# Packed query loads and a changed order of steps in a one-core linear-attention and mixture-of-depths kernel

## Chip, cores and metric

The kernel runs on one core of a Trainium2 chip. The metric is the time of one execution on the device in microseconds (us); smaller is better. All numbers below are of this one core.

## What is computed

The reference is a block-wise linear attention with a decay for each head, followed by a layer that sends the 128 best tokens of each of four batches through a two-matrix network. Cut to what matters, with B=4 batches, H=8 heads, S=768 tokens, D=64:

```python
for b in range(nb):                       # 12 blocks of 64 tokens
    intra = einsum('bhic,bhjc->bhij', qb, kb) * Dmask      # lam ** (i - j), i >= j
    intra = einsum('bhij,bhjd->bhid', intra, vb)
    inter = einsum('bhid,bhde->bhie', qb * lam_pow, kv_state)
    out[:, :, sl] = intra + inter
    kv_state = lam_block * kv_state + einsum('bhsd,bhse->bhde', kb * rev_pow, vb)
x = out.transpose(0, 2, 1, 3).reshape(B, S, 512)
scores = x @ w_gate
for b in range(B):
    top = the 128 tokens of batch b with the highest scores
    y = relu(x[b, top] @ w1) @ w2          # 512 -> 1024 -> 512
    out[b, top] = x[b, top] + sigmoid(scores[b, top])[:, None] * y
```

## The kernel before

The work is cut into 24 groups of 128 tokens (two blocks of 64), six groups to a batch; NT is 6, NG is 24. The engines' queues are written out by hand, in program order: the loop over g at L591 is one step for each group, and each step holds pieces of several groups, so that the engines overlap.

**Loads.** `load(g)` (L61) issues three DMAs on SyncE's queue (SP), one each for q, k and v of a group: 128 tokens on 128 partitions, 8 heads of 64 numbers beside each other, so every piece that is contiguous in memory is 256 bytes. Groups 0 to 2 are loaded ahead of everything, 3 to 5 in the prologue, and step g issues `load(g + 6)`; each name has 7 buffers. From step 4 to step 11 a step also issues `load_weights` (L81) behind its loads on the same queue: the four quarters of `w1_sb` in steps 4 to 7, the four of `w2_sb` in steps 8 to 11. Stores of the output go through ScalarE's queue (L315).

**A group's attention.** `keys_decayed` (L182) multiplies k by powers of the decay on GpSimd (tile `kd`). `transposes` (L191) turns q and k with TensorE: four 128x128 transposes of q into the PSUM tile `tq`, four of k into the upper halves of the two PSUM tiles `pu`; ScalarE copies them out as `qT` (L203) and `kT` (L206). `queries_decayed` (L209) makes `qs` on GpSimd. `scores` (L218) and `from_states` (L271) are 64x64 products on quarters of the array into `po`; `masked` (L229) multiplies the scores by the mask on VectorE (`p`); `from_scores` (L286) adds the rest of `po`. `state_products` (L241) fills the lower halves of `pu`; `decay_state` (L252, GpSimd, `decayed`) and `next_state` (L260, VectorE, `state`) carry the state on. `pu` has a single buffer (L54), so `state_products` of the next group waits until `next_state` and the copies of `kT` have read it. A 64x64 product in float32 stands in the profile as two matmuls and two weight loads.

**Order in a step.** Step g runs, on TensorE, `from_scores(g)`, `scores(g+1)`, `from_states(g+1)`, `state_products(g+2)`, perhaps an expert's `gate`, `transposes(g+2)`, then the pieces put into this step, and the transposed row of scores `row` (L340, tile `pb`). On GpSimd it runs `decay_state`, `keys_decayed(g+3)`, `queries_decayed(g+2)`, `decay_state`, and what pieces issue there.

**Choice of tokens and expert.** `gate_scores` (L325), `row`, `compare` and `compare_older` count for each token how many beat it. `places` (L394) has two parts: `ranks` (VectorE, tile `hit`) and `tokens` (six small products `pk` on TensorE, then the token numbers `tok` on VectorE). `expert` (L430) gathers the chosen rows into `xs` with an indirect DMA on GpSimd (`fetch`, L438), transposes them (`gate`, L446, `pt`), and has 16 pieces: eight of `hidden` (tile `ph`, L478, which reads all four quarters of `w1_sb`) and eight of `back` (`py`, L492); the last writes `y` back with an indirect DMA (L504). `plan(b)` (L525) lays these into later steps by `put(step, key, piece)`: for batches 0 to 2, with s = 6(b+1), ranks go to step s+1, tokens and the gather to step s+1 with keys 5 and 6, the gate to step s+3 and the pieces to steps from s+3 on. For the last batch all of it follows step 23. `row`, `tq`, `pt`, `pk`, `ph` and `py` share two PSUM banks, handed out in turn by `bank` (L163); an expert's `ph` or `py` holds one of them.

Of the kernel before, what the change touches and what calls it, by code (L numbers as in the profile page):

```python
# [17 lines left out]
def kernel(  # L18
# [12 lines left out]
    nc = tc.nc  # L31
# [11 lines left out]
    NGR = (CAP + 127) // 128  # L43
    NG = B * NT
    AHEAD = 6
    assert D == 64 and H % 2 == 0 and S % L == 0 and HD == 512 and F % 512 == 0
    assert 0 <= CAP < S

# [12 lines left out]
    def load(g):  # L61
        b, c = divmod(g, NT)
        rows = slice(c * L, (c + 1) * L)
        tiles = []
        for name, src in (("qn", q), ("kn", k), ("vn", v)):
            t = ld.tile([128, H, D], FP32, name=name)
            nc.sync.dma_start(out=t[:], in_=src[b, :, rows, :].rearrange("h p d -> p h d"))
            tiles.append(t)
        loaded[g] = tiles
# [46 lines left out]
    if CAP % 128:  # L116
# [4 lines left out]
            out=in_cap[:], in_=in_cap[:], compare_op=ALU.is_gt, fill=0.0,  # L121
            base=CAP % 128, pattern=[[0, 1]], channel_multiplier=-1,
        )
    half = [slice(0, C), slice(C, 2 * C)]

    mask = const.tile([128, 2, NHP, C], FP32, name="mask")
# [34 lines left out]
    def bank(shape, name, hold=False):  # L163

        tag = next(t for t in banks if t not in held)
        banks.remove(tag)
        banks.append(tag)
        if hold:
            held.append(tag)
        return ps_m.tile(shape, FP32, name=name, tag=tag)  # L170
# [11 lines left out]
    def keys_decayed(g):  # L182
        kd = att.tile([128, H, D], FP32, name="kd")
        nc.gpsimd.tensor_tensor(  # L184
            out=kd[:], in0=loaded[g][1][:],
            in1=kpow[:].rearrange("p a b -> p (a b)").unsqueeze(2).broadcast_to([128, H, D]),
            op=ALU.mult,
        )
        kds[g] = kd

    def transposes(g):  # L191

        tq = bank([128, NHP, L], "tq")
        tk = [u[:, NHP * D :].rearrange("p (a i) -> p a i", i=L) for u in us[g]]
        W = NHP // 2
        for i, dst in ((0, tq), (1, None)):
            for hp in range(NHP):
                nc.tensor.transpose(  # L198
                    dst[:, hp, :] if i == 0 else tk[hp // W][:, hp % W, :],
                    in_=loaded[g][i][:, 2 * hp : 2 * hp + 2, :], identity=ident[:],  # L200
                )
        qT = att.tile([128, NHP, L], FP32, name="qT")
        nc.scalar.copy(out=qT[:], in_=tq[:])  # L203
        kT = att.tile([128, NHP, L], FP32, name="kT")
        for i in range(2):
            nc.scalar.copy(out=kT[:, i * W : (i + 1) * W, :], in_=tk[i])  # L206
        qTs[g], kTs[g] = qT, kT

    def queries_decayed(g):  # L209
        qs = att.tile([128, NHP, L], FP32, name="qs")  # L210
        nc.gpsimd.tensor_tensor(  # L211
            out=qs[:], in0=qTs[g][:], in1=qpow[:].rearrange("p a c i -> p a (c i)"), op=ALU.mult
        )
        qss[g] = qs
# [14 lines left out]
    def masked(g):  # L229
        p = att.tile([128, 2, NHP, C], FP32, name="p")  # L230
        nc.vector.tensor_tensor(  # L231
            out=p[:].rearrange("p a b i -> p a (b i)"),
            in0=pos[g][:, :, 1].rearrange("p a b i -> p a (b i)"),
            in1=mask[:].rearrange("p a b i -> p a (b i)"), op=ALU.mult,
        )
        ps_[g] = p

    def start_u(g):
        us[g] = [ps_u.tile([128, 512], FP32, name=f"pu{c}") for c in range(2)]

    def state_products(g):  # L241
        vn, kd = loaded[g][2], kds.pop(g)
        for hp, hh, c in quarters():
            if c == 1 and g % NT == NT - 1:
                continue
            h = 2 * hp + hh
            nc.tensor.matmul(  # L247
                us[g][c][half[hh], hp * D : (hp + 1) * D], lhsT=kd[half[c], h, :],
                rhs=vn[half[c], h, :], start=True, stop=True, skip_group_check=True,
            )  # L250
# [86 lines left out]

    rows_, beatens, toks, upto = {}, {}, {}, {}

    def row(g):  # L340

        b, t = divmod(g, NT)
        if t == 0:
            rows_[b] = mod.tile([128, S], FP32, name="sc_row", tag="sc_row")
            beatens[b] = mod.tile([128, NT, NT + 1], FP32, name="beaten")
            nc.gpsimd.memset(beatens[b][:], 0.0)
            upto[b] = {n: n for n in range(NT)}
        pb = bank([128, L], "pb")
        nc.tensor.transpose(
            pb[:], in_=scs[b][:, t : t + 1].broadcast_to([128, 128]), identity=ident[:]  # L350
        )
        nc.scalar.copy(out=rows_[b][:, t * L : (t + 1) * L], in_=pb[:])

        cmp = mod.tile([128, S], BF16, name="cmp")
        nc.vector.scalar_tensor_tensor(
            out=cmp[:, :L], in0=pb[:], scalar=scs[b][:, t : t + 1], in1=not_before[:],
            op0=ALU.is_equal, op1=ALU.mult, accum_out=beatens[b][:, t, NT : NT + 1],
        )

# [158 lines left out]
    def put(step, key, piece):  # L518
        later.setdefault(step, []).append((key, piece))
# [5 lines left out]
    def plan(b):  # L525
        last = b == B - 1
        s = (b + 1) * NT
        ranks, tokens = places(b)
        if last:

            def last_row():
                compare_older(NG - 1)
                row(NG - 1)
                compare(NG - 1)
                ranks()

            put(s, 35, last_row)
            put(s, 85, tokens)
        else:
            ranked[s + 1] = ranks  # L540
            put(s + 1, 5, tokens)
        for i in range(NGR):
            s = max(s, busy_until[0])
            fetch, gate, pieces = expert(b, i)
            if s + 3 >= NG:
                s = max(s, NG)
                put(s, 86, fetch)
                put(s + 1, 0, gate)
                for j, piece in enumerate(pieces):
                    put(s + 2, j, piece)  # L550
                busy_until[0] = s + 3
                continue
            put(s + 1, 6, fetch)
            gates[s + 3] = gate

            whole = s + 9 <= NG
            counts = [2, 3, 3, 3, 3, 2] if whole else [1, 1, 1]
            assert len(pieces) == 16
            where = [(s + 3 + i, 10 * (j + 1)) for i, n in enumerate(counts) for j in range(n)]
            where = [w for w in where if w[0] < NG]  # L560
            where += [(NG, 10 * (j + 1)) for j in range(len(pieces) - len(where))]
            for (step, key), piece in zip(where, pieces):
                put(step, key, piece)
            busy_until[0] = s + 6 if whole else NG

    keys_decayed(0)
    start_u(0)
    transposes(0)
    queries_decayed(0)
    keys_decayed(1)  # L570
    state_products(0)
    next_state(0)
    decay_state(1)
# [1 line left out]
    decay_state(2)  # L575
    for g in range(3, AHEAD):
        load(g)
    start_u(1)
    transposes(1)
    queries_decayed(1)  # L580
    keys_decayed(2)
    scores(0)
    from_states(0)
    state_products(1)
    masked(0)
    next_state(2)
    decay_state(3)
    next_state(3)
# [2 lines left out]
    for g in range(NG):  # L591
        if g + AHEAD < NG:
            load(g + AHEAD)
        if 0 <= g - NT + 2 < n_w:
            load_weights(g - NT + 2)
        if g >= 2 * NT and kept:
            store_kept()
        if g + 2 < NG:
            decay_state(2 * g + 4)
        if g + 3 < NG:  # L600
            keys_decayed(g + 3)
        from_scores(g)
        outputs(g)
        if g + 1 < NG:
            scores(g + 1)
            from_states(g + 1)
            masked(g + 1)
        if g in ranked:
            ranked.pop(g)()
        if g % NT == 0 and g > 0 and NGR:  # L610
            compare_older(g - 1)
        if g + 2 < NG:
            start_u(g + 2)
            state_products(g + 2)
        if g in gates:
            gates.pop(g)()
        if g + 2 < NG:
            transposes(g + 2)
            queries_decayed(g + 2)
            next_state(2 * g + 4)  # L620
            decay_state(2 * g + 5)
        gate_scores(g)
        pieces = later.pop(g, [])

        rows = [r for r in {NG - 2: [g - 1, g], NG - 1: []}.get(g, [g - 1]) if r >= 0 and NGR]
        if g % NT == 0:
            for r in rows:
                row(r)
        else:
            in_order(pieces)  # L630
            for r in rows:
                row(r)
        if g + 2 < NG:
            next_state(2 * g + 5)
        for r in rows:
            compare(r)
        if g % NT == 0:
            in_order(pieces)
        if g % NT == NT - 1 and NGR:
            plan(g // NT)  # L640
# [35 lines left out]
```

## Time and profile before

| | |
|---|---|
| median of 3 runs | 188.24 us (187.86 to 188.97) |
| profiled execution | 189.73 us, of which the profile's span covers 188.0 us |
| granted TensorE clock, mean | 0.962 |
| TensorE busy, matmul / weight load | 153.5 us (82%) / 124.9 us (66%), 3520 of each |
| VectorE / ScalarE / GpSimd busy | 110.6 us (59%) / 68.0 us (36%) / 103.4 us (55%) |
| DMA | 80898 packets, 32.23 MB, mean 171 GB/s; 75616 packets under 512 B |
| last chain by engine | TensorE 56%, issue 16%, GpSimd 10%, VectorE 9%, DMA 3%, ScalarE 3% |

The span starts at 0 with the first instruction. Step g begins where the 32 matmuls of L289 for group g begin: step 0 at 15.66 us, step 1 at 22.56, step 2 at 27.15, step 7 at 51.99, step 8 at 59.75, step 9 at 66.34, step 10 at 72.42, step 23 at 153.77. After 154 us TensorE works through what is left of the third expert, then the whole of the fourth. In a timeline row, the first two numbers are the start and the length, a form is out<-in, xN counts merged instructions, and the square bracket holds the idle time of that engine just before, with what ended it. "issue" means idle for no reason that the profile shows. A DMA's row is its issue; the time to landing is listed apart.

### The profile page before, as it was taken

Reading aid. Unit: us, or ns where it says so; the run is one execution under the profiler, and the core shown is the slowest. Engines: PE = TensorE matmul, PEld = TensorE weight load, DVE = VectorE, ACT = ScalarE, POOL = GpSimd, SP = SyncE. Lnnn points to the kernel's source line nnn. Section 1 sums busy time; section 2 is a strip of 40 time slices with the busy share of each in tenths; the row PEclk is TensorE's granted clock in tenths of the full one; section 3 lists DMA queues with packets and bytes.
Section 4 is the critical chain, followed back from the end, with each engine's and each line's share of the span. In section 5 each row is a group of like instructions: output and inputs, shape, how many; then the busy total and the mean of one; then the engine's idle time right before and its main releaser. Section 6 shows DMA issues by size and latency. Waiting matters only on the chain.

```text
span 188.0 us, 8090 instructions
## 1 busy us (share of the span) xinstructions
PE 153.5 (82%) x3520; PEld 124.9 (66%) x3520; DVE 110.6 (59%) x357; ACT 68.0 (36%) x185; POOL 103.4 (55%) x110
## 2 busy tenths in 40 slices
PE   0957886876674799989799599999899969989980
PEld 0737775765564699988367399995667859549630
DVE  3903345866998378757873646749957689530000
ACT  2222253643344155536225333554425533111100
POOL 4386387867876686576756933768578500111002
PEclk9999699999999579999999969999999999999999
DMA  5999999899999999998999899411121211011001
GB/s 112 223 228 216 233 250 234 196 257 239 257 266 249 274 241 266 245 250 259 344 296 225 220 250 228 104 59 61 58 56 64 112 59 59 0 56 56 0 0 56
DMA packets 80898, 32.23 MB, mean 171 GB/s; under 512 B 75616, under 2 KB 75616, under 8 KB 80864
## 3 DMA queue, kind: packets, MB, share of 16 engines
q1 hardware_dynamic: 76688, 23.34, 56.1%
q10 hardware_dynamic: 3536, 6.30, 9.8%
q0 software_dynamic: 640, 2.10, 3.4%
q8 instruction: 27, 0.44, 1.0%
q14 instruction: 7, 0.06, 0.1%
HBM read 24.38 MB, written 7.34 MB: 169 GB/s over the span
## 4 chain that ended last, share of the span: by engine, by line
PE 56%; issue 16%; POOL 10%; DVE 9%; DMA 3%; ACT 3%; POOLq 1%; ACTq 0%; DVEq 0%
PE ph L478 11%; PE py L492 10%; PE pu L247 7%; PE tq L198 6%; PE po L289 6%; POOL qs L211 6%; PE po L278 5%; PE po L224 5%; PE pu L198 3%; POOL decayed L257 3%; ACT qT L203 3%; DMA lam_b<-in_lam_dram 2%; DVE cmp L365 2%; DMA out_dram<-y,tok 2%; DVE state L268 1%
## 5 line engine op out<-in xcount | busy, mean ns | idle before, releaser
L211 POOL TENSOR_TENSOR qs<-qT,qpow 128x512 f32<-128x512 f32 x24 | 31.3, 1303 | 27.6 <-ACT qT L203 26.0
L257 POOL TENSOR_TENSOR decayed<-state,decay 128x256 f32<-128x256 f32 x40 | 37.1, 927 | 16.7 <-DVE state L268 13.8
L478 PE MATMUL ph<-xsT,w_sb 128*128 128x128 f32 x256 | 31.1, 278 | 0.7 <-ACT xsT L454 0.7
L268 DVE TENSOR_TENSOR state<-pu,decayed 128x256 f32<-128x256 f32 x40 | 16.9, 422 | 24.3 <-ACT kT L206 17.7
L478 PEld LDWEIGHTS ph<-xsT,w_sb 128*128 128x128 f32 x256 | 29.8, 193 | 1.1 <-ACT xsT L454 0.9
L365 DVE TENSOR_SCALAR_CACHE_REDUCE cmp<-sc_row,sc 128x128 bf16<-128x128 f32 (+3 forms) x66 | 29.9, 497 | 0.0
L492 PE MATMUL py<-w_sb,hs 128*128 128x512 f32 x64 | 29.4, 599 | 0.4 <-ACT qT L203 0.4
L203 ACT COPY qT<-tq 128x512 f32<-128x512 f32 x24 | 14.0, 585 | 42.6 <-PE tq L198 41.4
L184 POOL TENSOR_TENSOR kd<-kn,kpow 128x512 f32<-128x512 f32 x24 | 26.0, 1082 | 3.0 <-DVE kpow L138 3.0
L328 DVE CUSTOM_DVE_ANT_0 xg<-x_b,wg_b 128x512 f32<-128x512 f32 x24 | 25.9, 1077 | 0.0
L247 PE MATMUL pu<-vn,kd 64*64 64x64 f32 x704 | 20.9, 237 | 3.5 <-DVE state L268 2.8
L278 PE MATMUL po<-state,qs 64*64 64x64 f32 x704 | 18.0, 225 | 7.0 <-issue 4.5
L231 DVE TENSOR_TENSOR p<-po,mask 128x512 f32<-128x512 f32 x24 | 16.5, 687 | 10.1 <-PE po L278 10.1
L198 PE MATMUL tq<-ident,qn 128*128 128x128 f32 x96 | 17.8, 315 | 5.6 <-DMA qn<-in_q_dram 4.9
L224 PE MATMUL po<-qT,kT 64*64 64x64 f32 x768 | 17.8, 228 | 5.0 <-issue 5.0
L247 PEld LDWEIGHTS pu<-vn,kd 64*64 64x64 f32 x704 | 17.7, 147 | 4.7 <-DVE state L268 1.8
L278 PEld LDWEIGHTS po<-state,qs 64*64 64x64 f32 x704 | 15.1, 138 | 8.1 <-issue 5.1
L492 PEld LDWEIGHTS py<-w_sb,hs 128*128 128x128 f32 x64 | 11.4, 190 | 11.9 <-issue 10.8
L289 PEld LDWEIGHTS po<-vn,p 64*64 64x64 f32 x768 | 14.5, 144 | 7.0 <-issue 4.2
L224 PEld LDWEIGHTS po<-qT,kT 64*64 64x64 f32 x768 | 15.2, 141 | 5.7 <-issue 5.7
L198 PE MATMUL pu<-ident,kn 128*128 128x128 f32 x96 | 17.1, 305 | 2.0 <-DVE state L268 1.9
L289 PE MATMUL po<-vn,p 64*64 64x64 f32 x768 | 17.9, 235 | 0.3 <-DVE p L231 0.3
(53 smaller groups left out, 151.4 us busy)
## 6 DMA issues: line engine op xcount, KB each, us to landing
qn<-in_q_dram SPq DMA_DIRECT2D x24, 256.0 KB, 5.3
kn<-in_k_dram SPq DMA_DIRECT2D x24, 256.0 KB, 5.5
vn<-in_v_dram SPq DMA_DIRECT2D x24, 256.0 KB, 5.7
out_dram<-x_b ACTq DMA_DIRECT2D x18, 256.0 KB, 3.7
w_sb<-in_moe_w_dram SPq DMA_DIRECT2D x8, 512.0 KB, 5.8
out_dram<-x_b ACTq DMA_DIRECT2D x2, 768.0 KB
wg_b<-in_moe_w_gate_dram SPq DMA_DIRECT2D x1, 256.0 KB
xs<-out_dram,tok POOLq DMA_INDIRECT x4, 4.5
```

Of the source, the lines that this page charges most:

```text
L184: nc.gpsimd.tensor_tensor(out=kd[:], in0=loaded[g][1][:], in1=kpow[:].rearrange("p a b -> p (a b)").unsqueeze(2).broadcast_to([128, H, D]) ...
L198: nc.tensor.transpose(dst[:, hp, :] if i == 0 else tk[hp // W][:, hp % W, :], in_=loaded[g][i][:, 2 * hp : 2 * hp + 2, :], identity=ident[:],)
L211: nc.gpsimd.tensor_tensor(out=qs[:], in0=qTs[g][:], in1=qpow[:].rearrange("p a c i -> p a (c i)"), op=ALU.mult)
L224: nc.tensor.matmul(po[half[c], hh, 1, hp, :], lhsT=kT[half[hh], hp, half[c]], rhs=qT[half[hh], hp, half[c]], start=True, stop=True, skip_g ...
L247: nc.tensor.matmul(us[g][c][half[hh], hp * D : (hp + 1) * D], lhsT=kd[half[c], h, :], rhs=vn[half[c], h, :], start=True, stop=True, skip_g ...
L257: nc.gpsimd.tensor_tensor(out=t[:], in0=states[n][:], in1=decay[:], op=ALU.mult)
L278: nc.tensor.matmul(pos[g][half[hh ^ c], hh, 0, hp, :], lhsT=qs[half[hh], hp, half[c]], rhs=states[n][half[hh], hp, :], start=(hp == 0), st ...
L289: nc.tensor.matmul(pos[g][half[hh ^ c], hh, 0, hp, :], lhsT=p[half[c], hh, hp, :], rhs=vn[half[c], 2 * hp + hh, :], start=(hp == 0 and (2 ...
L328: nc.vector.tensor_tensor_reduce(out=xg[:], in0=x_bs[b][:, t].rearrange("p a b e -> p (a b e)"), in1=wg_b[:], scale=1.0, scalar=0.0, op0=A ...
L365: nc.vector.tensor_scalar(out=cmp[:, : cols.stop - cols.start], in0=rows_[b][:, cols], scalar1=scs[b][:, t : t + 1], scalar2=None, op0=op, ...
L478: nc.tensor.matmul(ph[:, fc % 4, :], lhsT=w1_sb[:, dc, fc * 128 : (fc + 1) * 128], rhs=keep["xsT"][:, dc, :], start=(dc == 0), stop=(dc == ...
L492: nc.tensor.matmul(py[:], lhsT=keep["hs"][:, fc, :], rhs=w2_sb[:, fc, :], start=(fc == 0), stop=(fc == NFC - 1),)
```

## The change

1. For groups 0 to 11 (`PACKED`, two batches), q is loaded in another shape: partition (hh, a, t) of the tile holds eight neighbouring tokens 8t to 8t+7 of head 2a+hh, 2 KB in one piece. It takes two DMAs of 64 partitions, one for each hh, in place of one of 128. k and v stay as they were.
2. For these groups the four transposes of q become 16 products of 64x64, on two quarters of the array (rows hh to columns hh), with the identity `ident2` as moving operand, and the copy to `qT` reads PSUM with a step of 64 elements to put the tokens in order again.
3. For groups 0 and 1, k is transposed into a `bank` tile of its own (`tk`), not into `pu`, and the prologue runs `scores(0)` ahead of `state_products(0)`, and `from_states(0)` and `masked(0)` ahead of `state_products(1)`.
4. `tokens` and `fetch` of batch 0 move from step 7 to step 8; its gate stays in step 9. Those of batches 1 and 2 stay in their step, with keys 25 and 26, so behind two pieces of `back`.
5. The `row` of groups 22 and 23 uses the `pu` tiles, not a `bank`; `start_u` is called once more for that.

```diff
+    PACKED = 2 * NT
+            if name == "qn" and g < PACKED:
+                qsrc = src[b, :, rows, :].rearrange("(a h) (t s) d -> h a t (s d)", h=2, s=8)
+                for hh in range(2):
+                    nc.sync.dma_start(
+                        out=t[half[hh]].rearrange("p s d -> p (s d)"), in_=qsrc[hh]
+                    )
+                tiles.append(t)
+                continue
...
     def transposes(g):
         tq = bank([128, NHP, L], "tq")
-        tk = [u[:, NHP * D :].rearrange("p (a i) -> p a i", i=L) for u in us[g]]
...
+        if g < PACKED:
+            for s in range(8):
+                for hh in range(2):
+                    nc.tensor.matmul(
+                        tq[half[hh]].rearrange("p a i -> p (a i)")[:, s * 64 : s * 64 + 64],
+                        lhsT=loaded[g][0][half[hh], s, :], rhs=ident2[half[hh], :],
+                        start=(s == 0), stop=True, skip_group_check=True,
+                    )
+            nc.scalar.copy(
+                out=qT[:].rearrange("p a (t s) -> p a t s", s=8),
+                in_=tq[:].rearrange("p a i -> p (a i)").rearrange(
+                    "p (s a t) -> p a t s", s=8, a=NHP
+                ),
+            )
+        else:
...
+        if g < 2:
+            tk = bank([128, NHP, L], "tk")
+            tk = [tk[:, i * W : (i + 1) * W, :] for i in range(2)]
+        else:
+            tk = [u[:, NHP * D :].rearrange("p (a i) -> p a i", i=L) for u in us[g]]
...
-    def row(g):
+    def row(g, pb=None):
...
-        pb = bank([128, L], "pb")
+        if pb is None:
+            pb = bank([128, L], "pb")
+        pb = pb[:, :L]
...
-                row(NG - 1)
+                row(NG - 1, us[NG][1])
...
-            put(s + 1, 5, tokens)
+            where = (s + 1, 25) if b > 0 else (s + 2, 5)
+            put(*where, tokens)
...
-            put(s + 1, 6, fetch)
+            put(s + 1, 26, fetch) if i > 0 or b > 0 else put(s + 2, 6, fetch)
...
     keys_decayed(0)
-    start_u(0)
     transposes(0)
     queries_decayed(0)
     keys_decayed(1)
+    scores(0)
+    start_u(0)
     state_products(0)
...
-    start_u(1)
     transposes(1)
+    from_states(0)
+    masked(0)
     queries_decayed(1)
     keys_decayed(2)
-    scores(0)
-    from_states(0)
+    start_u(1)
     state_products(1)
-    masked(0)
...
+        if g + 2 <= NG:
+            start_u(g + 2)
         if g + 2 < NG:
-            start_u(g + 2)
             state_products(g + 2)
...
-                row(r)
+                row(r, us[NG][0] if r == NG - 2 else None)
```

More of the change, by code (lines that the diff above doesn't have):

```diff
@@ L45 @@
     AHEAD = 6
+    PACKED = 2 * NT
+    half = [slice(0, C), slice(C, 2 * C)]
     assert D == 64 and H % 2 == 0 and S % L == 0 and HD == 512 and F % 512 == 0
@@ L123 @@
         )
-    half = [slice(0, C), slice(C, 2 * C)]
     mask = const.tile([128, 2, NHP, C], FP32, name="mask")
@@ L193, in transposes @@
         tq = bank([128, NHP, L], "tq")
-        tk = [u[:, NHP * D :].rearrange("p (a i) -> p a i", i=L) for u in us[g]]
-        W = NHP // 2
-        for i, dst in ((0, tq), (1, None)):
+        qT = att.tile([128, NHP, L], FP32, name="qT")
+        if g < PACKED:
[13 more added lines that the diff above has]
+        else:
             for hp in range(NHP):
                 nc.tensor.transpose(
-                    dst[:, hp, :] if i == 0 else tk[hp // W][:, hp % W, :],
-                    in_=loaded[g][i][:, 2 * hp : 2 * hp + 2, :], identity=ident[:],
-                )
-        qT = att.tile([128, NHP, L], FP32, name="qT")
-        nc.scalar.copy(out=qT[:], in_=tq[:])
+                    tq[:, hp, :], in_=loaded[g][0][:, 2 * hp : 2 * hp + 2, :], identity=ident[:]
+                )
+            nc.scalar.copy(out=qT[:], in_=tq[:])
+        W = NHP // 2
+        if g < 2:
[3 more added lines that the diff above has]
+            tk = [u[:, NHP * D :].rearrange("p (a i) -> p a i", i=L) for u in us[g]]
+        for hp in range(NHP):
+            nc.tensor.transpose(
+                tk[hp // W][:, hp % W, :], in_=loaded[g][1][:, 2 * hp : 2 * hp + 2, :],
+                identity=ident[:],
+            )
         kT = att.tile([128, NHP, L], FP32, name="kT")
@@ L347, in row @@
             upto[b] = {n: n for n in range(NT)}
-        pb = bank([128, L], "pb")
+        if pb is None:
+            pb = bank([128, L], "pb")
+        pb = pb[:, :L]
         nc.tensor.transpose(
-            pb[:], in_=scs[b][:, t : t + 1].broadcast_to([128, 128]), identity=ident[:]
+            pb, in_=scs[b][:, t : t + 1].broadcast_to([128, 128]), identity=ident[:]
         )
-        nc.scalar.copy(out=rows_[b][:, t * L : (t + 1) * L], in_=pb[:])
+        nc.scalar.copy(out=rows_[b][:, t * L : (t + 1) * L], in_=pb)
         cmp = mod.tile([128, S], BF16, name="cmp")
         nc.vector.scalar_tensor_tensor(
-            out=cmp[:, :L], in0=pb[:], scalar=scs[b][:, t : t + 1], in1=not_before[:],
+            out=cmp[:, :L], in0=pb, scalar=scs[b][:, t : t + 1], in1=not_before[:],
             op0=ALU.is_equal, op1=ALU.mult, accum_out=beatens[b][:, t, NT : NT + 1],
```

## Prediction

> **What bounds the kernel now.** I read first the page's DMA rows, then the DMA view of two windows, then the timelines around the first expert (59 to 76 us) and the prologue, then the chain of waits.
>
> The page: mean busy share of the 16 DMA engines in 40 slices of 4.7 us, then packets, MB and share by queue (q1 is SP's, q10 ScalarE's, q8 carries instructions).
>
> ```profile
> DMA  5999999899999999998999899411121211011001
> ...
> q1 hardware_dynamic: 76688, 23.34, 56.1%
> q10 hardware_dynamic: 3536, 6.30, 9.8%
> ...
> q8 instruction: 27, 0.44, 1.0%
> ```
>
> The engines are full from 5 to 118 us. SP's packets count out: 72 loads x 1024 pieces = 73,728, 128 for the gate row, 512 and 1,024 for the weights; 1,296 are left, which is 16 for each of SP's 81 DMAs.
>
> Prices, from the DMA view of 30 to 45 us (loads alone on q1) and of 125 to 165 us (quiet, stores on q10):
>
> ```profile
> q1 hardware_dynamic: 9981, 2.52, 76.6%
> ```
>
> ```profile
> q10 hardware_dynamic: 864, 1.57, 10.6%
> ```
>
> 0.766 x 16 x 15 us / 9981 = 18.4 ns for a 256-byte packet. 0.106 x 16 x 40 us / 864 = 78 ns; 96 of the 864 are the small ones (six stores x 16), about 9 ns each, so a 2 KB packet takes 87 ns.
>
> Full engines hurt only where someone waits for what they bring late. The last quarter of w1 is issued in step 7, behind the loads of group 13, and the first expert needs it in step 9. SP's timeline, the landing times in 60 to 72 us, and TensorE's timeline:
>
> ```profile
> 61.51 0.91 SPq L83 DMA_DIRECT2D w_sb<-in_moe_w_dram  x1
> ```
>
> ```profile
> w_sb<-in_moe_w_dram SPq DMA_DIRECT2D x2, 512.0 KB, 6.4
> ```
>
> ```profile
> 70.37 2.02 PE L478 MATMUL ph<-xsT,w_sb 128*128 128x128 f32 x16
> ```
>
> It lands at 61.51 + 6.4 = 67.9 and is read at 70.37: 2.5 us to spare, the smallest margin of any load I found. TensorE itself loses time in three ways. The timeline shows it waiting in the prologue and for tokens and rows:
>
> ```profile
> 12.26 0.69 PE L198 MATMUL pu<-ident,kn 128*128 128x128 f32 x2 [1.95 <-DVE state L268]
> ```
>
> ```profile
> 59.35 0.30 PE L417 MATMUL pk<-ids,hit 128*128 128x2 bf16 x6 [2.46 <-DVE hit L406]
> ```
>
> ```profile
> 96.34 0.30 PE L417 MATMUL pk<-ids,hit 128*128 128x2 bf16 x6 [0.39 <-DVE hit L406]
> ```
>
> ```profile
> 135.82 0.30 PE L417 MATMUL pk<-ids,hit 128*128 128x2 bf16 x6 [0.77 <-DVE hit L406]
> ...
> 153.51 0.32 PE L349 MATMUL pb<-ident,sc 128*128 128x128 f32 x1 [1.45 <-DVE cmp L355]
> ```
>
> And the chain of waits has stretches in which TensorE waited for nothing shown:
>
> ```profile
> 42.63 1.58 issue
> ...
> 48.48 1.29 issue
> ...
> 53.23 1.19 issue
> ...
> 105.36 2.18 issue
> ```
>
> With 80.56 (0.71) and 92.73 (1.22) these six sum to 8.2 us. From 44.2 to 49.8 and from 49.8 to 54.4 about 127 matmuls and as many weight loads pass, and q8's 27 packets are 16 KB each: these are pauses at instruction pages, 4.6 to 5.6 us apart.
>
> [...]
>
> **The change, part by part.** *The packed load.* The memory side of each half is 4 heads (98,304 numbers apart) x 16 x 2 KB; the heads cannot be merged with the 16. Its slowest dimension is 4, the tile's is 64[...], both halves on the same four engines. Each of these then carries 128/4 = 32 packets of 2 KB a group, 32 x 87 ns = 2.78 us, where it carried 64 x 18.4 ns = 1.18 us. That is 1.61 us more a group, 19.3 us for twelve; the other twelve engines get 1.18 us less. A DMA that spans all 16 (k, v, weights) lands with the slowest. So the last quarter of w1, behind all twelve packed groups, lands 19.3 us later, less the time these engines now stand idle. The table by stage (length, busy time of each engine, granted clock, DMA share, GB/s) has only these two stretches below a share of 0.97:
>
> ```profile
> 32.40:36.60 4.20, 3.61 (x123) 3.12 (x121) 3.23 (x9) 2.69 (x9) 3.45 (x5) 1.00 0.79 184
> ...
> 41.30:46.50 5.20, 3.62 (x123) 3.22 (x121) 3.56 (x9) 2.34 (x8) 4.14 (x4) 1.00 0.95 234
> ```
>
> 0.21 x 4.2 + 0.05 x 5.2 = 1.1 us idle. L478 then waits 19.3 - 1.1 - 2.5 = 15.7 us. Behind it on TensorE stand the next row and from_scores(10), so the other engines run dry.
>
> Bounds: none if k is 16; at the loaded rate of 2 KB packets (window 30 to 45, q10: 121 ns with the small ones taken off) 32 x 121 - 1180 = 2.69 us a group, 32 us. I take the quiet rate[...]. SP issues four DMAs a group instead of three[...]. As late keys also pace steps 3 to 8 (group period on four engines 2.78 + 2 x 1.18 = 5.1 us bare, 5.9 with a store of 8 x 87 ns; the steps take 4.2 to 5.5), everything earlier than the weights is under this cover.
>
> *Transposes as products.* 8 TensorE instructions become 64 a group, so 56 more. Sixteen matmuls on two quarters (L247 in group 11) took 0.46 us to the next instruction in the chain, so 32 take 0.93 against 0.60: 0.33 us x 10 groups = 3.3 us, hidden under the load wait, on the path without it. Copy to qT with a stepped read: between 0 and +0.59 us (twice the row) a group; I take 0. A gain is excluded, as the same 512 elements pass.
>
> *Prologue.* Key transposes no longer wait 1.95 us for the state. What is late next is GpSimd's own row of kd(1), decayed, qs, kd(2); that leaves about 1.0 us. Under load wait: nothing, since k and v of group 1 come later.
>
> *Tokens of batch 0.* 2.46 us on TensorE and the row that GpSimd's memset delays go. By the step lengths 51.99 to 59.75 and 59.75 to 66.34 against about 5.3, 2.0 + 1.3 = 3.3 us are at stake. But the gather now stands behind decayed of step 8, which ends at 68.5 in the old clock, 65.2 in the shortened one, lands 5 us later at 70.2, and the gate reads at 69.0: net +1.2 us (-3.3 to +3). Hidden by the wait for w1 while that is there. *Batches 1 and 2:* two back products cover the 0.39 and 0.77 us. *Rows:* 0.25 us, since sc(22) is ready at 153.2 and pb waited to 153.5. These three are behind the weights and count: -1.4 us. The order of instructions on the engines says what moves with the pieces: VectorE's tok_f and tok of batch 0 go one step down with the tokens, the gather goes past the memset of `beaten` and a step of GpSimd's work; for batches 1 and 2 GpSimd's order is as before, and masked(0) keeps its place on VectorE.
>
> Sum: 189.73 + 15.7 - 1.4 = 204.0 for an execution like the profiled one, which is 1.5 above the median of the runs: 202.5, which I round to 202.
>
> **Rivals.** *The loads do spread over 16 engines, and TensorE's pages decide.* For: [...] Ten groups x 56 = 560 instructions = 2.2 pages, at 4.9 us a page up to 10.7 us[...]. 188.24 + 5.4 + 1.2 - 1.0 - 1.4 = 192.4. [...] *The other side: loads on 16 engines relieve the fetch of instructions.* A group's q takes 8 x 87 = 0.70 us instead of 1.18, 5.8 us less by group 12; the six pauses lie before 118 us, where the queues are full; after that the chain has one of 0.43 us. 188.24 - 8.2 + 3.3 + 1.2 - 1.0 - 1.4 = 182.1. It decides from k = 8 on: 16 x 87 = 1.39 us is 0.21 above the old 1.18, within the (2.5 + 1.1)/12 = 0.3 us of slack; with k = 4 it cannot. *The edits cancel:* 188.
>
> **Numbers.** Four engines 0.61, own range 195 to 207. Low: the pauses after step 9 (0.71 + 1.22 + 2.18) go[...], and a packet takes 80 ns (2.7 us less). High: 100 ns a packet, 5.0 us more. Page-bound 0.18, relieved 0.15, cancelled 0.06. The range leaves out the relieved case and the far tails: 187 to 207. Within 0.5% is about what a measurement of this kernel can tell from no change. Faster 0.15, same 0.06, slower 0.79.
>
> **What would show it.** SP's packets: 65,744 + 24k, 65,840 with four engines, 66,128 with sixteen. A wait of L478 for w_sb near 70 us, GpSimd waiting for kn in steps 3 to 8, and a DMA share of 5 to 7 tenths, not 9, before 80 us. Wrong: 16 small packets a packed DMA, w_sb landing before 70 us.

## The result, and the profile after

| | before | changed |
|---|---|---|
| median of 4 runs, same chip | 188.13 us | 205.74 us (204.84 to 210.71) |
| ratio, 95% interval | | 1.0895 (1.082 to 1.097) |
| the same once more, in another series | 186.52 us | 204.25 us, ratio 1.0944 (1.088 to 1.101) |

The changed kernel is slower by 17.6 us; 202 with a range of 187 to 207 was forecast. Medians and ranges are of all runs; the ratios here and below compare only the runs within 1.5% of the fastest of the same kernel. The first profiled execution lasted 210.71 us, 5 us over its own median. All readings below, where the first profile is not named, are therefore from a second profile of the same program, whose execution lasted 203.34 us with a span of 201.6, against 189.73 and 188.0 before: 13.6 us more. The other 4.0 us of the 17.6 lie between executions: the one profiled before was 1.6 us above its median, this one 0.9 below the median of its series, and that median 1.5 below the first.

The DMA share by slices of 5.0 us, SP's and the instructions' queues (packets, MB, share of 16 engines), and the chain that ended last by engine (SPq is SP's queue), in which the kernel before had 56% for TensorE, 3% for DMA and nothing for SP:

```profile
DMA  1779848667796789999999999991113121011001
...
q1 hardware_dynamic: 65840, 23.34, 51.3%
...
q8 instruction: 30, 0.49, 1.1%
...
PE 39%; SPq 15%; DMA 14%; POOL 10%; issue 9%; DVE 7%; ACT 3%; POOLq 1%; ACTq 0%; DVEq 0%
```

65,840 is 65,744 + 24 x 4: four small packets a packed DMA. The forecast's k, the number of engines of one packed DMA, is 4: in the first profile, by the times of the packets from 25 to 70 us, at most five 2 KB packets of q are in flight in 99% of the time that there are any, most often four. The packets of a pair's second half, issued at 31.16 us, begin there at 34.59, as those of the first half end (34.64). From 5 to 70 us the engines together are busy 75% of the time (by slices 40 to 90%), and yet SP stands. Its timeline for two packed groups and the last quarter of w1 (the two packed DMAs of a group are merged in one row):

```profile
44.79 5.08 SPq L73 DMA_DIRECT2D qn<-in_q_dram  x2
49.97 0.41 SPq L78 DMA_DIRECT2D kn<-in_k_dram  x1
50.47 0.53 SPq L78 DMA_DIRECT2D vn<-in_v_dram  x1
51.05 3.96 SPq L73 DMA_DIRECT2D qn<-in_q_dram  x2
...
81.98 1.01 SPq L94 DMA_DIRECT2D w_sb<-in_moe_w_dram  x1
```

A pair mostly holds SP for 3.6 to 5.1 us. From the issue at 33.78 to that at 56.41 four groups take 22.63 us, 5.66 each; 5.1 bare and 5.9 with a store had been worked out. In that stretch the table by stage (length, busy time of each engine, granted clock, DMA share, GB/s) has a share of 0.70, where before it was 1.02 from 20 to 60 us:

```profile
33.78:56.41 22.63, 17.76 (x633) 15.49 (x631) 13.01 (x39) 9.44 (x28) 14.97 (x16) 0.96 0.70 170
```

The last quarter of w1 was issued at 81.98 instead of 61.51. By the times of its packets, which no row here shows, the last one ends at 86.9 us, against 67.2 before: 19.7 us later (forecast 19.3 - 1.1 = 18.2). But the first expert doesn't wait for it. TensorE's timeline in step 9:

```profile
85.27 1.08 PE L484 MATMUL pt<-ident,xs 128*128 128x128 f32 x4 [4.89 <-DMA xs<-out_dram,tok]
86.28 1.97 PE L208 MATMUL tq<-ident,qn 64*64 64x64 f32 x32
88.18 1.12 PE L232 MATMUL pu<-ident,kn 128*128 128x128 f32 x4
89.09 2.51 PE L512 MATMUL ph<-xsT,w_sb 128*128 128x128 f32 x16
```

Row L512 (L478 before) has no wait in front of it: the gathered rows were there only at 85.1 us, and the last packet of w1 had ended 2.2 us before ph. And TensorE works slowly behind that wait; the granted clock is the third figure from the right:

```profile
85.00:87.00 2.00, 1.74 (x18) 1.43 (x20) 0.70 (x2) 0.61 (x2) 0.00 (x0) 0.50 1.16 293
87.00:89.00 2.00, 2.00 (x28) 1.88 (x25) 0.32 (x2) 0.70 (x3) 0.00 (x0) 0.50 1.10 210
89.00:91.00 2.00, 2.00 (x15) 2.00 (x13) 1.41 (x3) 0.71 (x2) 1.98 (x2) 0.68 0.92 282
91.00:93.00 2.00, 2.00 (x99) 1.83 (x100) 0.95 (x5) 0.85 (x3) 0.74 (x1) 1.00 1.15 255
```

Where the time went is read from the starts of the steps (L321, before L289):

| step starts at | 2 | 5 | 7 | 9 | 10 | 14 | 16 | 23 | span |
|---|---|---|---|---|---|---|---|---|---|
| before | 27.15 | 41.37 | 51.99 | 66.34 | 72.42 | 99.36 | 113.93 | 153.77 | 188.0 |
| changed | 34.65 | 50.67 | 65.41 | 77.32 | 91.65 | 116.96 | 128.09 | 167.29 | 201.6 |
| later by | 7.5 | 9.3 | 13.4 | 11.0 | 19.2 | 17.6 | 14.2 | 13.5 | 13.6 |

Eleven us are lost up to the start of step 9, where late loads set the pace, 8.2 in step 9, and 5 of these come back by step 16. GpSimd's waits (total, times, longest) show the first part; before it waited for no kn at L184:

```profile
POOL kd L193 <- DMA kn<-in_k_dram: 20.1, 7, 5.5
```

The chain of waits shows a second way by which a late load passes on. At 57.3 a store on ScalarE's queue is released by the landing of v, whose issue SP had delayed, and the copy to qT stands behind that store. The trace gives both DMAs the same completion semaphore (a counter of landings, number 101 here): its last count for v came at 57.30 us, and the store was issued at 57.37.

```profile
50.47 6.83 DMA vn<-in_v_dram
...
57.37 0.34 ACTq L347
...
57.81 0.59 ACT qT L213
...
58.47 1.28 POOL qs L243
```

### The profile page after: what moved, and what is told of

It reads as the page before. It is cut to its first block, busy times and chain, and to the rows that moved or that the text cites. A ratio compares the mean times of both kernels' runs of the same rounds, so it can differ in the third digit from the quotient of the medians.

```text
span 209.0 us, 8773 instructions
## 1 busy us (share of the span) xinstructions
PE 167.1 (80%) x3856; PEld 137.0 (66%) x3856; DVE 110.2 (53%) x357; ACT 68.5 (33%) x185; POOL 103.0 (49%) x110
## 3 DMA queue, kind: packets, MB, share of 16 engines
q1 hardware_dynamic: 65840, 23.34, 49.6%
## 4 chain that ended last, share of the span: by engine, by line
PE 38%; SPq 17%; issue 11%; DMA 11%; DVE 10%; POOL 7%; ACT 3%; POOLq 1%; ACTq 0%; DVEq 0%
SPq L73 12%; PE ph L512 9%; PE py L526 8%; SPq L78 4%; PE pu L279 4%; DMA vn<-in_v_dram 4%; PE tq L208 3%; PE tq L221 3%; PE po L321 3%; DMA kn<-in_k_dram 3%; POOL qs L243 3%; POOL decayed L289 3%; DMA xs<-out_dram,tok 2%; PE po L310 2%; PE po L256 2%
## 5 line engine op out<-in xcount | busy, mean ns | idle before, releaser
L289 POOL TENSOR_TENSOR decayed<-state,decay 128x256 f32<-128x256 f32 x40 | 36.6, 916 | 14.9 <-DVE state L300 14.7
L512 PE MATMUL ph<-xsT,w_sb 128*128 128x128 f32 x256 | 32.0, 283 | 0.7 <-ACT xsT L488 0.7
L526 PE MATMUL py<-w_sb,hs 128*128 128x512 f32 x64 | 31.7, 632 | 0.4 <-ACT qT L224 0.4
L512 PEld LDWEIGHTS ph<-xsT,w_sb 128*128 128x128 f32 x256 | 30.7, 199 | 1.1 <-ACT xsT L488 0.9
L208 PE MATMUL tq<-ident,qn 64*64 64x64 f32 x384 | 20.8, 272 | 8.8 <-DMA qn<-in_q_dram 7.3
L208 PEld LDWEIGHTS tq<-ident,qn 64*64 64x64 f32 x384 | 19.3, 185 | 9.4 <-DVE lam_p L153 5.9
L360 DVE CUSTOM_DVE_ANT_0 xg<-x_b,wg_b 128x512 f32<-128x512 f32 x24 | 24.9, 1037 | 0.0
L213 ACT COPY qT<-tq 128x512 f32<-128x512 f32 x12 | 7.0, 585 | 50.8 <-PE tq L208 38.4
L256 PE MATMUL po<-qT,kT 64*64 64x64 f32 x768 | 16.7, 227 | 2.9 <-ACT kT L238 2.8
L321 PEld LDWEIGHTS po<-vn,p 64*64 64x64 f32 x768 | 13.6, 135 | 6.7 <-issue 3.4
L337 ACT COPY x_b<-po 64x256 f32<-64x256 f32 x48 | 17.6, 366 | 0.6
L321 PE MATMUL po<-vn,p 64*64 64x64 f32 x768 | 16.9, 226 | 0.5 <-DVE p L263 0.5
```

The costliest lines, as they stand in the source:

```text
L208: nc.tensor.matmul(tq[half[hh]].rearrange("p a i -> p (a i)")[:, s * 64 : s * 64 + 64], lhsT=loaded[g][0][half[hh], s, :], rhs=ident2[half ...
L289: nc.gpsimd.tensor_tensor(out=t[:], in0=states[n][:], in1=decay[:], op=ALU.mult)
L321: nc.tensor.matmul(pos[g][half[hh ^ c], hh, 0, hp, :], lhsT=p[half[c], hh, hp, :], rhs=vn[half[c], 2 * hp + hh, :], start=(hp == 0 and (2 ...
L360: nc.vector.tensor_tensor_reduce(out=xg[:], in0=x_bs[b][:, t].rearrange("p a b e -> p (a b e)"), in1=wg_b[:], scale=1.0, scalar=0.0, op0=A ...
L512: nc.tensor.matmul(ph[:, fc % 4, :], lhsT=w1_sb[:, dc, fc * 128 : (fc + 1) * 128], rhs=keep["xsT"][:, dc, :], start=(dc == 0), stop=(dc == ...
L526: nc.tensor.matmul(py[:], lhsT=keep["hs"][:, fc, :], rhs=w2_sb[:, fc, :], start=(fc == 0), stop=(fc == NFC - 1),)
```

## The experiments

Theory A is the forecast's: a packed load ran on four engines. Theory B: the products on TensorE, with their instructions, are what costs. Theory C: the later gather of batch 0 costs by itself. Ratios are to the kernel before on the same chip.

**1. Sixteen engines.**

```diff
-                qsrc = src[b, :, rows, :].rearrange("(a h) (t s) d -> h a t (s d)", h=2, s=8)
+                qsrc = src[b, :, rows, :].rearrange("(a h) (t s) d -> h t a (s d)", h=2, s=8)
...
-                    "p (s a t) -> p a t s", s=8, a=NHP
+                    "p (s t a) -> p a t s", s=8, a=NHP
```

> Only the order of the partitions inside a half is changed, from (head, token block) to (token block, head), and the read of the copy to qT with it: the slowest dimension of the memory side becomes 16. Theory A (the forecast: a packed load ran on four engines): SP's packets rise from 65,840 to 66,128, the pair of packed issues no longer holds SP for about 4 us, steps 1 to 9 come back to the pace of before, the last quarter of w1 lands before 70 us instead of at 87.5, and the time is 182 to 189 us. Theory B (the 56 more TensorE instructions a group and the stepped copy are what costs): nothing of that matters, 200 us or more. Theory C (the later gather of batch 0 costs by itself): the wait of pt for xs stays at 4 to 5 us, and the time is 189 to 193.

Measured: 195.31 us, ratio 1.034 (1.025 to 1.043).

```profile
q1 hardware_dynamic: 66128, 23.34, 52.6%
```

```profile
29.50 2.75 SPq L73 DMA_DIRECT2D qn<-in_q_dram  x2
32.36 0.52 SPq L78 DMA_DIRECT2D kn<-in_k_dram  x1
32.98 0.53 SPq L78 DMA_DIRECT2D vn<-in_v_dram  x1
33.56 2.82 SPq L73 DMA_DIRECT2D qn<-in_q_dram  x2
```

Sixteen small packets a DMA, 4.3 us from pair to pair in the mean of four instead of 5.7, w1 landed at 68.6, step 9 at 68.93 (2.6 after the kernel before). The copy to qT takes 587 ns, as before. So going from four to sixteen engines takes away 10 us of the 17. The edit also changes the sequence of addresses, but that did not change the price of the packets: in sum SP's took 0.526 x 16 x 194.3 = 1635 us here and 0.513 x 16 x 201.6 = 1655 us in the changed kernel. What changed is over how many engines they are spread. The time is above A's range all the same, and above C's: 3.4% stay, and in step 9 pt waits 5.3 us for xs, so C is alive. Behind that wait pt, pu and ph take 1.09, 1.04 and 2.23 us, against 0.59, 0.44 and 1.85 in the kernel before, at a clock of 1.00 (67.8 to 72.4 us).

**2. Eight engines**, by four DMAs of 32 partitions, on top of edit 1.

```diff
-                for hh in range(2):
+                for i in range(4):
                     nc.sync.dma_start(
-                        out=t[half[hh]].rearrange("p s d -> p (s d)"), in_=qsrc[hh]
+                        out=t[32 * i : 32 * i + 32].rearrange("p s d -> p (s d)"),
+                        in_=qsrc[i // 2, 8 * (i % 2) : 8 * (i % 2) + 8],
                     )
```

> As the run with sixteen, but four DMAs of 32 partitions, whose memory side has a slowest dimension of 8. Theory A: eight engines carry 16 packets of 2 KB a group, about 1.4 us against 1.18 before and 2.78 with four engines, which is inside the slack: 16 + 16 = 32 small packets a group, SP's packets 66,128 again (4 x 8 a group), and a time within 3 us of the run with sixteen (184 to 191). If the number of engines were not what counts, but the number of DMAs or of packets, it would stand near 205.

Measured: 201.26 us, ratio 1.074 (1.064 to 1.084). The packets are 66,128, as for eight engines; the time is a miss. From the chain:

```profile
31.59 3.91 DMA out_dram<-x_b
35.52 0.67 SPq L73
36.23 0.67 SPq L73
36.95 4.21 DMA kn<-in_k_dram
```

Where nothing held SP, the four DMAs of a group took 2.86 us of it, a pair in run 1 only 1.18; and here a packed load waited for the landing of a store. Groups follow at 6.0 us, at a DMA share of 0.70. The run mixes two things, number of engines and number of DMAs, and does not tell what eight engines alone would cost.

**3. Load and products alone**, in the kernel before; k goes into `pu` as it did.

```diff
+            if name == "qn" and g < PACKED:
+                qsrc = src[b, :, rows, :].rearrange("(a h) (t s) d -> h a t (s d)", h=2, s=8)
...
+        if g < PACKED:
+            for s in range(8):
+                for hh in range(2):
+                    nc.tensor.matmul(
...
+        tk = [u[:, NHP * D :].rearrange("p (a i) -> p a i", i=L) for u in us[g]]
```

> The kernel before with the packed load and the products alone, none of the changes of order (batch 0's tokens in step 7, its gather and gate as before). Theory A as recorded: the last quarter of w1 decides, lands near 87 us, the first ph waits for w_sb, and the time stays at 203 to 207. Theory C: the 5.1 us wait for xs came on top of the late loads, so without it the time falls to 200 or 201, and ph waits for w_sb 1 to 3 us instead.

Measured: 207.33 us, ratio 1.108 (1.097 to 1.119). Here w1 is waited for. Among TensorE's waits:

```profile
PE ph L508 <- DMA w_sb<-in_moe_w_dram: 3.5, 1, 3.5
```

Without the wait for xs the time did not fall: in the total this is A (0.3 us above its range), but w1 is only the last of the late loads.

**4. The order alone.**

```diff
-    PACKED = 2 * NT
+    PACKED = 0
```

> The changed kernel with PACKED = 0: plain loads and transposes for all groups, and the changes of order alone. The sums of the forecast: prologue -1.0, tokens of batch 0 net +1.2 (-3.3 to +3), tokens of the other batches and the row -1.4, so 187 us (183.5 to 189). Theory C: pt waits for xs by about 4 us in step 9, and the time is 189 to 191.

Measured: 190.50 us, ratio 1.010 (1.005 to 1.016): slower by 1%, as C says, and outside the forecast's range. Step 0 begins 2.26 us earlier than before; step 9 takes 13.82 us instead of 6.08. TensorE's timeline, and the table by stage before and behind that wait:

```profile
72.44 1.09 PE L484 MATMUL pt<-ident,xs 128*128 128x128 f32 x4 [5.93 <-DMA xs<-out_dram,tok]
```

```profile
64.20:66.40 2.20, 2.20 (x113) 2.05 (x112) 2.03 (x7) 1.57 (x6) 2.20 (x2) 1.00 0.93 192
72.20:78.10 5.90, 5.67 (x33) 5.52 (x33) 2.54 (x7) 1.86 (x5) 2.72 (x2) 0.58 0.93 217
```

From pt to the row after ph it takes 77.86 - 72.44 = 5.42 us, against 72.22 - 69.00 = 3.22 before: the low clock adds 2.2 us to a wait of 5.9.

**5. Tokens and gather of batch 0 back in step 7, with four engines** (run twice).

```diff
-            where = (s + 1, 25) if b > 0 else (s + 2, 5)
+            where = (s + 1, 25) if b > 0 else (s + 1, 5)
...
-            put(s + 1, 26, fetch) if i > 0 or b > 0 else put(s + 2, 6, fetch)
+            put(s + 1, 26 if i > 0 or b > 0 else 6, fetch)
```

> The changed kernel with one edit undone: tokens and gather of batch 0 are back in step 7. Theory A (with four engines the landing of w1 at about 87 us sets the start of the first expert): pt no longer waits for xs, but the first ph waits 1 to 4 us for w_sb, TensorE waits about 2.4 us for hit, and the time moves by less than 1.5% (ratio to the kernel before 1.075 to 1.10, where the changed kernel had 1.0895). Theory C (the wait of 5.1 us for xs and the low clock behind it cost by themselves): 5 to 7 us less, a ratio of 1.05 to 1.06.

Measured: ratio 1.128 (1.115 to 1.141), above both. It was repeated beside the changed kernel:

> The changed kernel itself, on the chip of the next run, to compare the two. A ratio near its first one, 1.08 to 1.10.

> The changed kernel with batch 0's tokens and gather back in step 7, once more and on the same chip as the changed kernel. If the late loads of four engines cover the later gather, as forecast, the two ratios are within 1% of each other; if the gather's wait of 5 us costs by itself, this one is 2 to 3% lower; the first run of it (1.128) says that it is higher, by a mechanism that no theory here has.

Measured on one chip: changed kernel 1.0944 (1.088 to 1.101), tokens back 1.0939 (1.086 to 1.102). The later gather costs nothing while four engines carry q. What takes its place (timeline of the second run):

```profile
85.46 1.24 PE L512 MATMUL ph<-xsT,w_sb 128*128 128x128 f32 x6
88.16 1.38 PE L512 MATMUL ph<-xsT,w_sb 128*128 128x128 f32 x10 [1.45 <-DMA w_sb<-in_moe_w_dram]
```

ph starts with the three quarters that are there and stands until 88.1 for the fourth; in the changed kernel ph started at 89.1, with all of w1 there and the rows late. Two late things share one wait. Why the first run of it stood at 1.128 stays open; the repeat did not show it.

**6. Sixteen engines and tokens back.** Edits 1 and 5 together.

> The kernel with sixteen engines, with tokens and gather of batch 0 back in step 7. In that kernel w1 landed at 68.6, so nothing covers the wait of 5.3 us for xs in step 9, behind which the granted clock was 0.6 or so for six us. Theory C: the wait goes, and the time falls by 4 to 7 us against the run with sixteen, a ratio of 0.995 to 1.015. If the products and the stepped copy (theory B) are what is left of the loss, the ratio stays at 1.025 to 1.035.

Measured: 193.13 us, ratio 1.026 (1.009 to 1.042). The middle is where B put it, and the interval reaches into C's: undecided.

**7. Order alone, tokens back.** Edits 4 and 5.

> No packed groups, and tokens and gather of batch 0 in step 7: of the change there are left the prologue's order, the tokens of batches 1 and 2 behind two pieces, and the last rows. The forecast has -1.0 and -1.4 for these, so a ratio of 0.987. From the trace of the order alone, steps 0 to 2 started 2.3 us earlier than before and steps 10 to 16 gave back 4.3 us: if these last, 183 to 186 us, a ratio of 0.97 to 0.985. If the start of the first expert is set by w1, which lands at 67 to 70 us, the gain of the prologue is lost there and the ratio is 0.995 to 1.

Measured: 187.84 us over 20 runs, ratio 0.985 (0.976 to 0.994). Against run 4 (1.010) the later gather costs 2.5%, about 4.8 us, where no late packed load covers it. That size is rough: the ratio rests on two of the 20 runs, the medians of all runs give 0.993 here and 1.001 for run 4 (0.8% apart), and the two profiled executions are 3.3 us apart. All three have the same sign; the size is 1.5 to 5 us. Steps 0 to 8 begin 2.7 to 3.2 us earlier than before, and 2.7 of that are lost in step 9, for w1:

```profile
70.09 1.38 PE L512 MATMUL ph<-xsT,w_sb 128*128 128x128 f32 x10 [2.66 <-DMA w_sb<-in_moe_w_dram]
```

**8. w1 early, with four engines**: edit 5, and

```diff
-        if 0 <= g - NT + 2 < n_w:
-            load_weights(g - NT + 2)
+        if 1 <= g < 5:
+            load_weights(g - 1)
+        if 8 <= g < 12:
+            load_weights(g - 4)
```

> As the changed kernel with the tokens back, and with the four quarters of w1 issued in steps 1 to 4 instead of 4 to 7, ahead of three packed groups each. Theory A as recorded (w1 behind all packed groups is the wait that decides): it lands near 70 us, ph no longer waits for it, and the time falls by 3 us or more against the same kernel with w1 late. Theory D (every load of the first twelve groups is late, and w1 is only the last of them): the same bytes pass the same four engines, groups 7 to 10 come up to 5 us later, and the time is within 1% of that kernel.

Measured: 208.35 us, ratio 1.112 (1.096 to 1.127); run 5 on that chip 210.22. w1 landed at 75.8 and nothing waited for it, but it was only 1.9 us faster, inside the noise. This speaks for D, that all loads are late; it does not exclude a small share for w1.

**9. Products alone**, from q as loaded before.

```diff
+            if i == 0 and g < 2 * NT:
+                for h in range(H):
+                    for hh in range(2):
+                        nc.tensor.matmul(
+                            tq[half[hh]].rearrange("p a i -> p (a i)")[:, h * C : h * C + C],
+                            lhsT=loaded[g][0][half[hh], h, :], rhs=ident2[half[hh], :],
+                            start=(h == 0), stop=True, skip_group_check=True,
+                        )
+                continue
```

> The kernel before with one thing changed: in groups 0 to 11 the four transposes of q are 16 products on two quarters, from q as it was loaded before; the copy to qT is the plain one. The heads stand in another order in qT, so the scores are of other pairs than in the reference; number and size of all operations are as in the changed kernel. In the run with sixteen engines and the tokens back, load and products together still cost 4.2% against the same order without them (ratios 1.026 and 0.985). Theory B1 (products on the path, no more pages felt): 10 groups at 0.46 us, a ratio of 1.015 to 1.03. Theory B2 (their 560 more instructions also bring two more pauses for pages): 1.03 to 1.045. Theory E (the products are hidden by the waits for loads, and the 4% are the packed load itself): under 1.01.

The kernel leaves the heads in another order, so its scores are of other pairs. Measured: 191.49 us, ratio 1.027 (1.021 to 1.032), 5.0 us: B1. The chain has 0.91 us for one group's products (row "PE tq L208 x30" of the changed kernel) and 0.59 for the four transposes before: 0.32 more, where 0.33 was forecast, so ten groups make 3.2 us of the 5.0. The rest may lie with three more packets of instructions (30 on q8, before 27); it was not separated.

**10. A version faster than before and changed**: run 7 with each quarter of w1 and w2 one step earlier.

```diff
-        if 0 <= g - NT + 2 < n_w:
-            load_weights(g - NT + 2)
+        if 0 <= g - NT + 3 < n_w:
+            load_weights(g - NT + 3)
```

> The changes of order alone with the tokens back (ratio 0.985), and every quarter of w1 and w2 issued one step earlier. There TensorE waited 2.7 us in step 9 for the last quarter of w1[...]. If that wait is what holds the prologue's gain back: it goes, and the ratio falls to 0.965 to 0.98. If keys and values that now stand behind the weights are late in its place: 0.985 to 1.0.

Measured: 181.50 us, ratio 0.977 (0.971 to 0.982). In its profile (an execution of 188.0 us, well above its median, so only this row is used) ph in step 9 follows without a wait, as intended. The interval overlaps that of run 7 (0.976 to 0.994), so a gain over run 7 is not shown:

```profile
67.48 2.02 PE L512 MATMUL ph<-xsT,w_sb 128*128 128x128 f32 x16
```

## Why the prediction was right, and where it was not

The measured 205.74 us lie in the range, 3.7 above the forecast of 202. The mechanism named first, loads on four engines, is what costs; where the time is lost was forecast wrongly in part.

**Four engines: right.** That four engines follow from a slowest dimension of 4 was the author's estimate, which no run had shown by then. With that dimension at 4 the packets show k = 4 (65,840 of SP's), at 8 in run 2 they show 8 (65,744 + 48 x 8 = 66,128), at 16 in run 1 they show 16 (66,128). Which engines they were no row shows. That k and v land late with q shows in the first profile: from 20 to 60 us four to six 256-byte packets of SP are in flight in 27% of the time, where before it was 8%. The size was close too: with run 7 (0.985) and run 9 (1.027) multiplied, order and products alone would stand at 1.011; the same with four engines stands at 1.094 (run 5, second time), 8.2% more, about 15 us, where 15.7 had been worked out for the wait. This is more than the 10 us between four and sixteen engines, probably because with sixteen the later gather and the products are no longer covered by late loads. That the parts multiply is an assumption, and the 0.985 rests on two runs; with 0.993 the same sum gives 7.3%, and runs 3 and 9 (1.108 / 1.027), which do not need run 7, give 7.9%. For the packed load on sixteen engines the sum gives 1.034 / (1.010 x 1.027) = 0.997 from run 1 and 1.026 / 1.011 = 1.014 from run 6, with an interval of 1.6% to each side there: no cost that these runs can tell from nothing.

**Where it is paid: wrong.** "L478 then waits 15.7 us" failed. The wait is 0 in the changed kernel, and 1.5 or 3.5 us with the gather in its old place. The step took the weights as the only load that anyone waits for. But the same delay had grown with every packed group before them, and 11.0 us of it were paid by the start of step 9. Nor were w1's 2.5 us the smallest margin: by the completion counts in the trace before, the keys of groups 0 to 3 landed only 0.2 to 1.1 us before `kd` read them (group 0 at 5.92, read at 6.16), so the first late loads are paid at once. Of the signs named, the packets, GpSimd's waits for kn and the lower DMA share (0.74 in the mean before 80 us) came; the wait of L478 did not. The sentence that all earlier waits are under one cover saved the total: the 11.0 us paid before step 9 and the 15.7 did not add up (19.2 at step 10). That the end came so close is in part luck: at step 10 the delay was 19.2 us, where 15.7 was forecast, and 5.0 of it came back by step 16, where only the 0.39 of batch 1 was forecast; 13.6 at the end of the profile stands beside the forecast's 15.7 - 1.4 = 14.3.

**Tokens of batch 0: cover right, size too small.** For "net +1.2 us (-3.3 to +3)" run 4 against run 7 gives 4.8 us, or 1.5 to 5 (see there). The gate was put 4.5 us behind its start (70.2 against 69.0 - 3.3); it waited 5.93, and the forecast had nothing for TensorE's clock, 2.2 us more. The 3.3 at stake were also summed wrongly: 7.76 - 5.3 is 2.5, not 2.0, which makes them 3.8. The clock was low behind the two long waits: behind 4.89 us it was 0.50 from 85 to 89 us and 1.00 from 91, and behind 5.93 us (run 4) 0.58. Behind 2.66 us (run 7) it stayed at 1.00, but in run 9 it was 0.71 behind a pause of 2.54, and in the kernel before 0.50 from 61.0 to 67.8 us, after the wait of 2.46 for hit, so the length of a wait alone does not tell the clock here. That the us of the later gather were hidden with four engines is shown by the second time of run 5; that they count with sixteen is not shown, since run 6 is only 0.8% below run 1, inside the noise.

**Products: size per group right, total 5.0 instead of 3.3.** The stepped copy at nothing is right: 586 ns against 585. **Prologue:** -1.0 was too small; alone it brings 2.3 to 2.9 us at step 0 (runs 4 and 7), and under late loads no gain shows, as said: step 0 begins 1.7 us late. **Batches 1 and 2:** right; the delay shrinks by 0.7 in step 13 and 0.9 in step 19, where 0.39 and 0.77 were worked out. **Rows:** 0.25 us cannot be seen; the delay is 13.5 at step 23 and 13.6 at the end.

**The rivals.** Pages with sixteen engines (192.4) is the nearer one to what sixteen engines gave, 1.034 x 188.13 = 194.6, but its 4.9 us a page, of which it took half, were the author's estimate and nearly the distance between pauses (4.6 to 5.6 us); the six pauses in the kernel before last 1.4 us in the mean (by the packets' times a 16 KB packet of q8 ends from 0.6 us before to 0.7 us after the start of each), and runs 4 and 9 speak for the gather (1.010) and the products (1.027) as what is left. That sixteen engines relieve the fetch of instructions was not borne out: the packets of q1 took 1635 us in sum in run 1 against 0.561 x 16 x 188.0 = 1687 before, only 3% less, TensorE still waited 7.5 us for nothing shown (10.6 before), and the time was 194.6, not 182.1.

**Open.** In step 15 the delay falls by 3.8 us: that step took 9.50 us before, with a pause of 2.18, and 5.72 in the changed kernel. Relieved engines are not needed for it, since run 9 with its old loads takes the same 5.7. In the whole profile TensorE's waits for nothing shown sum to 10.6 us before and 2.6 in the changed kernel, so fewer pauses offset part of the late loads there. But with four engines too they are 9.6 in run 3 and 7.4 in the second profile of run 5, so this does not follow from the load. Why the pauses fall where they do was not shown.

## What to carry to other kernels

Before a load is packed into longer pieces, write down the slowest dimension of both of its sides: a rearrangement of the partitions that keeps all sizes, and costs nothing elsewhere, took that of the memory side from 4 to 16 and was worth 10 us here (ratio 1.0895 to 1.034, run 1). When a queue falls behind, work out its total delay once, and look for the waits from the first load on, not at the last one only. Count a wait of TensorE together with the clock behind it: behind 5.93 us it was 0.58, which added 2.2 us (run 4).

## What the hardware showed unexpectedly

With 30% of the DMA engines' time free (33.78 to 56.41 us), SP stood 3.6 to 5.1 us at a packed pair, and the loads of k and v behind it, sixteen small packets each, were issued only after it (pair at 44.79 for 5.08 us, k at 49.97). Twice as many DMAs on eight engines (run 2, 1.074) were nearly as slow as four engines (1.0895). A store on ScalarE's queue was issued (57.37 us) only when v's load on SP's, with the same completion semaphore, had landed (57.30). In the kernel before, a 2 KB packet of SP took 115 ns in the mean from 18 to 73 us (84 in the median), not the 87 of the quiet stretch.
